# Two sequence mixers in one kernel: x in four loads with the states in time order, part of B turned on TensorE, and a new order of all operations

## The chip, the cores and the metric

The kernel runs on one core of one Trainium2 chip. Its time is the device time of that core in microseconds (us). Of the kernel before, three runs are shown.

## What is computed

Two independent mixers read [1, 2048, 640] inputs in bf16, and their outputs stand side by side in a [1, 2048, 1280] result. Part A is a diagonal complex state-space model (S5): a projection by B, a linear recurrence over the 2048 rows, and a projection by C. Part B is a gated long convolution (H3): a four-tap convolution of k, times v, then a convolution with a filter as long as the sequence, by Fourier transforms, and times q.

```python
# part A
B_bar = ((Lam_bar - 1.0) / Lam)[:, None] * Bmat          # Lam_bar = exp(dt * Lam)
Bu = jnp.einsum("bld,pd->blp", x + 0j, B_bar)
for t in range(L):
    h = Lam_bar[None, :] * h + Bu[:, t, :]
y = 2.0 * jnp.einsum("blp,dp->bld", hseq, Cmat).real + x * Dskip[None, None, :]
# part B
for t in range(ks):                                      # ks = 4
    k_shift = k_shift + k_pad[:, t:t + S, :] * shift_k[:, ks - 1 - t][None, None, :]
kv = k_shift * v
y = irfft(rfft(kv, 2 * S) * rfft(ssm_k, 2 * S), 2 * S)[:, :S] + kv * ssm_D
out = q * y
```

## The kernel before

**Part A.** x comes by eight transposing loads of 256 rows (`load_x`, L525), so that a feature lies on each partition. The rows are taken in residue classes modulo 16, and `base` (L559) multiplies them by B: 400 matmuls of 512 columns, which read x at every second element. The ten state tiles (640 complex states, real and imaginary parts on 128 partitions) stand in `A` as [10 tiles, 16 residues, 130]. The recurrence is done by doubling: `up2`, `up1` and `up0` (with `rmm`, L580) add the state of an earlier residue, times a power of the transition held as a matrix in RR; `coarse` scans the 128 blocks that are left on VectorE (L654 to L665); `down` (L684, its eviction L700 on ScalarE or L702 on VectorE) spreads the result back in four levels. Where ScalarE evicts, an identity matmul (L682) adds the old value. `project` makes 16 output tiles of 128 rows (L719, 20 matmuls of 128x320 each); x times D (L711) is made beforehand from rows that are loaded again (L710), added at the eviction (L721), and stored (L725). B's first 128 rows come plain on ScalarE's DMA queue and are turned by TensorE transposes (L502), the rest in four transposing loads (L493).

**Part B.** k and v come by transposing loads (L774); the convolution is multiplications (L198 on VectorE, L199 on ScalarE), sums (L800) and a product with v (L801), on VectorE or GpSimd. The result goes to a buffer in DRAM (L807) and back in another layout (L817). Two halves of 320 channels follow. A first DFT stage (`s1`, for the filter "h" and the signal "k") is done wide (L836, 16 matmuls) or narrow (L841, 32 matmuls of half the rows and columns), as a flag of the operation says; it is evicted at L846. A second stage (L860, eviction L873) leaves both spectra in SBUF. `product` multiplies them in four blocks of each half: one operation of 128x2560 (L884, on VectorE alone), two in-place products of 128x1280 (L887), a difference (L889) and a sum (L891), these four on VectorE or GpSimd. All blocks share one buffer for the result of L884, so a block's L884 waits for the L889 of the block before. The inverse stages are L905 (eviction L910), which needs all four blocks of its half, and L926 (eviction with times q, L938), then the store.

**Order.** No scheduler runs on the device: each operation is recorded with the engines that could do it, and a table, `ORDER`, lists all operations by number, engine (S for SyncE's DMA queue, A ScalarE, V VectorE, G GpSimd, T TensorE, t for a narrow first stage) and PSUM bank. Each engine does its own in that order, and waits where a footprint in SBUF or a PSUM bank says so. TensorE's results lie in eight banks; an operation takes one or two.

Of the kernel before, what the change touches and what calls it, by code (L numbers as in the profile page):

```python
# [183 lines left out]
for _name, _n in (("A", 10 * 16 * 130), ("BT", 6400), ("RR", 5120), ("W", 4096), ("G", 8192), ("XT", 10240), ("AS", 10240),  # L184
# [153 lines left out]
def params(c):  # L338
# [7 lines left out]
    for k, src in enumerate((lam_re, lam_im, ldt_in)):  # L346
        rows = pr[10 * k:10 * k + 10, :]
        P.add("ld_par", {PSP: .1, PACT: .1}, lambda e, rows=rows, src=src: e.dma_start(
            out=rows.rearrange("p (a b) -> p a b", a=2), in_=bass.AP(src.tensor, 0, [[64, 10], [0, 2], [1, 64]])),
            outs=[tk[:, k:k + 1]], ins=[pr], nbytes=2560)  # L350
# [114 lines left out]
class PartA:  # L465
    def __init__(self, c):
        self.c = c
        v = c.v
        self.A = v("A").rearrange("p (j i s) -> p j i s", j=10, i=16)
        self.BT = []  # L470
        for n, lo in ((2, 0), (4, 1280), (4, 3840)):
# [6 lines left out]
        self.XP = v("XT").rearrange("p (g d s a) -> p d g a s", d=5, g=8, a=2)  # L478
# [3 lines left out]
    def load_B(self, k):  # L482
        c, P = self.c, self.c.P
        n, lo, row = ((2, 0, 0), (4, 1280, 128), (4, 3840, 384))[k]
        raw = c.v("T", 1280, 1280)
        for ri, src in ((0, c.ins["A_B_re"]), (1, c.ins["A_B_im"])):
            if k == 0:
                dst = raw[:, 640 * ri:640 * ri + 640]
                P.add("ld_Braw", {PACT: .1}, lambda e, dst=dst, src=src: e.dma_start(out=dst, in_=src[0:128, :]), outs=[dst], nbytes=128 * 1280)
                continue  # L490
            dst = c.v("BT", lo + 320 * n * ri, 320 * n).rearrange("p (d m) -> p d m", d=5)
            s = src[row:row + 64 * n, :].rearrange("p (d q) -> p d q", q=128)
            P.add(f"ld_B{k}", {PSP: 64 * n * .0055}, lambda e, dst=dst, s=s: e.dma_start_transpose(out=dst, in_=s), outs=[dst],  # L493
                  nbytes=64 * n * 1280)
        if k == 0:
            idn = c.I3[:, 0:128]
            for r in range(2):
                g, out, part = P.group(1), c.v("BT", 640 * r, 640), raw[:, 640 * r:640 * r + 640]

                def mm(e, B, part=part):  # L500
                    for d in range(5):
                        e.transpose(out=B.bitcast(bf16)[:, 128 * d:128 * d + 128], in_=part[:, 128 * d:128 * d + 128], identity=idn)  # L502
                P.add("turn_B", {PPE: .29}, mm, ins=[part, idn], group=g, nmm=5)
                P.add("ev_B", {PDVE: .5, PACT: .7}, lambda e, B, out=out: c.CP[e](out=out, in_=B.bitcast(bf16)[:, 0:640]), outs=[out], group=g)
# [15 lines left out]
    def load_x(self, g):  # L520

        c, P = self.c, self.c.P
        dst = c.v("XT", 1280 * g, 1280).rearrange("p (d t) -> p d t", d=5)
        s = self.x2.rearrange("(s r) (d q) -> r s d q", r=8, q=128)[min(ROW0[2 * g], ROW0[2 * g + 1])]
        P.add(f"ld_x{g}", {PSP: 1.4}, lambda e: e.dma_start_transpose(out=dst, in_=s), outs=[dst], nbytes=256 * 1280)  # L525
# [30 lines left out]
    def base(self, e, o, j, q):  # L556
        for d in range(5):
            for r in range(2):
                e.matmul(o[64 * r:64 * r + 64], lhsT=self.BT[j][:, r, d, :], rhs=self.XP[:, d, 2 * q:2 * q + 2], start=(d == 0),  # L559
                         stop=(d == 4), skip_group_check=True, tile_position=(0, 64 * r))  # L560

    def base_in(self, j, q):
        return [self.BT[j], self.c.v("XT", 2560 * q, 2560)]

    def up2(self, j0, q):
# [4 lines left out]
        def mm(e, B):  # L570
            for a in range(2):
                self.base(e, B[:, 512 * a:512 * a + 512], j0 + a, 2 + q)
        P.add(f"up2{q}_{j0}", {PPE: 10 * .216}, mm, ins=self.base_in(j0, 2 + q) + [self.BT[j0 + 1]], group=g, nmm=20)
        out = self.A[:, j0:j0 + 2, 8 + 4 * q:12 + 4 * q, 0:128]
        P.add(f"ev_up2{q}_{j0}", {PDVE: dve(1024), PACT: act(1024)},
              lambda e, B: c.CP[e](out=out, in_=B.rearrange("p (a i s) -> p a i s", a=2, s=128)), outs=[out], group=g)  # L576

    def rmm(self, e, o, n, j, lo, hi):
# [591 lines left out]
```

## Time and profile before

| | |
|---|---|
| three runs | 198.66, 199.42 and 200.72 us; median 199.42 |
| the profiled execution | span 199.3 us from first to last instruction, 0.1 under the median |
| busy share | TensorE 91%, VectorE 82%, ScalarE 68%, GpSimd 37% |
| mean granted TensorE clock | 0.991 |
| DMA | 30.15 MB, 151 GB/s on average |
| VectorE instructions / GpSimd instructions | 225 / 62 |

In the profile PE is TensorE's matmul stream, PEld its weight loads, DVE VectorE, ACT ScalarE, POOL GpSimd, and SP the queue that issues most DMA. A line such as L887 is a line of the kernel before. A group row gives the line, engine, operation, output and input shape and count, then busy time and the mean of one in ns, then the idle time of the engine just ahead of them with what ended it. A timeline row gives start and duration in us, and in brackets the idle time ahead. Matmuls are pipelined, so that the duration of one is longer than the distance to the next.

### The profile page before, as it was taken

To read this page: it belongs to the slowest core of one execution; us is meant where nothing else is said; L and a number is where in the kernel's file an instruction comes from. 1 tells how busy PE (TensorE), PEld (TensorE's weight loads), DVE (VectorE), ACT (ScalarE), POOL (GpSimd) and SP (SyncE) were. 2 spreads that over 40 slices of the span, in tenths; PEclk is the share of its full clock that TensorE was granted. 3 is DMA by queue.
4 is the path that set the end of the run, shared out by engine and by line. 5 is a ranking of instruction groups with operands and counts; after the bars stand their busy time and mean duration, and the time that the engine had idled before them with its cause. 6 is when DMAs were issued, how large, how long until landed. Compare 5 with 4: busy or idle time off the path is not lost.

```text
span 199.3 us, 7475 instructions
## 1 busy us (share of the span) xinstructions
PE 181.9 (91%) x3324; PEld 123.4 (62%) x3324; DVE 163.0 (82%) x225; ACT 135.8 (68%) x166; POOL 73.1 (37%) x62
## 2 busy tenths in 40 slices
PE   4979999999799999888959988999999999999992
PEld 1545555654468674665738654755767786797771
DVE  4705699599868979999898878989989999997941
ACT  3279988959888689998967889983877290192000
POOL 8399800590060050007270385299250004500050
PEclk9999999999999999999997999999999999999999
DMA  5999999999999999999892799028546732375785
GB/s 107 183 174 134 193 134 163 167 155 178 235 221 288 153 169 157 173 138 116 143 286 55 172 134 138 5 79 125 130 127 140 168 99 72 102 199 135 162 200 139
DMA packets 107738, 30.15 MB, mean 151 GB/s; under 512 B 102586, under 2 KB 107066, under 8 KB 107706
## 3 DMA queue, kind: packets, MB, share of 16 engines
q1 hardware_dynamic: 107418, 29.35, 84.0%
q8 instruction: 26, 0.43, 1.0%
q10 hardware_dynamic: 288, 0.33, 0.6%
q14 instruction: 6, 0.05, 0.1%
HBM read 10.99 MB, written 7.86 MB: 95 GB/s over the span
## 4 chain that ended last, share of the span: by engine, by line
PE 52%; DMA 14%; DVE 11%; ACT 11%; SPq 7%; issue 3%; ACTq 0%; DVEq 0%
PE acc L559 18%; PE acc L719 16%; ACT arena L873 6%; DMA arena<-in_A_x_dram 5%; PE acc L860 4%; PE acc L905 4%; SPq L767 4%; DMA arena<-in_B_k_dram 3%; DMA kv_rows<-arena 2%; ACT arena L846 2%; DMA arena<-in_A_B_re_dram 2%; PE acc L684 2%; PE acc L580 2%; DVE arena L721 2%; PE acc L926 2%
## 5 line engine op out<-in xcount | busy, mean ns | idle before, releaser
L559 PE MATMUL acc<-arena 128*64 128x512 bf16 x400 | 47.3, 389 | 1.5 <-DMA arena<-in_A_B_re_dram 1.1
L719 PE MATMUL acc<-arena 128*128 128x320 bf16 x320 | 45.7, 299 | 0.8 <-ACT arena L846 0.6
L873 ACT CAST arena<-acc 128x960 bf16<-128x960 f32 (+1 forms) x41 | 36.2, 916 | 9.2 <-PE acc L860 7.3
L719 PEld LDWEIGHTS <-arena 128*128 128x128 bf16 x320 | 30.3, 98 | 13.4 <-ACT arena L846 0.8
L559 PEld LDWEIGHTS <-arena 128*64 128x64 bf16 x400 | 24.4, 108 | 21.2 <-issue 2.6
L846 ACT CAST arena<-acc 128x1024 bf16<-128x1024 f32 x29 | 27.7, 1054 | 3.0 <-PE acc L836 2.3
L910 ACT CAST arena<-acc 128x1024 bf16<-128x1024 f32 x17 | 16.2, 1035 | 16.4 <-PE acc L905 16.4
L860 PE MATMUL acc<-arena 128*64 128x160 bf16 x512 | 23.7, 238 | 1.4 <-ACT arena L873 0.8
L887 POOL TENSOR_TENSOR arena<-arena 128x1280 bf16<-128x1280 bf16 x6 | 16.7, 2790 | 20.7 <-DVE arena L884 20.7
L860 PEld LDWEIGHTS <-arena 128*64 128x64 bf16 x512 | 18.3, 111 | 9.2 <-ACT arena L873 3.6
L702 DVE TENSOR_TENSOR arena<-acc,arena 128x1024 bf16<-128x1024 f32 (+1 forms) x15 | 17.2, 1166 | 2.4 <-PE acc L684 2.0
L836 PE MATMUL acc<-arena 128*64 128x128 bf16 x400 | 15.2, 227 | 4.3 <-DVE arena L721 2.1
L721 DVE TENSOR_TENSOR arena<-acc,arena 128x640 bf16<-128x640 f32 x16 | 13.2, 823 | 6.8 <-PE acc L719 5.7
L800 DVE TENSOR_TENSOR arena<-arena 128x2048 bf16<-128x2048 bf16 x14 | 17.1, 1220 | 1.0 <-ACT arena L199 0.8
L836 PEld LDWEIGHTS <-arena 128*64 128x64 bf16 x400 | 12.9, 115 | 6.6 <-DVE arena L721 2.2
L846 DVE CAST arena<-acc 128x1024 bf16<-128x1024 f32 x11 | 13.1, 1219 | 4.5 <-PE acc L836 3.9
L889 POOL TENSOR_TENSOR arena<-arena 128x1280 bf16<-128x1280 bf16 x3 | 7.8, 2609 | 19.6 <-DVE arena L887 19.5
L684 PE MATMUL acc<-arena 128*128 128x512 bf16 (+2 forms) x50 | 12.4, 337 | 0.8 <-ACT arena L873 0.7
L199 ACT ACTIVATE arena<-arena 128x2048 bf16<-128x2048 bf16 (+2 forms) x10 | 11.0, 1110 | 2.7 <-DMA arena<-in_B_k_dram 2.7
L884 DVE TENSOR_TENSOR arena<-arena 128x2560 bf16<-128x2560 bf16 x8 | 11.9, 1489 | 0.5 <-ACT arena L873 0.3
L711 POOL TENSOR_TENSOR arena<-arena 128x640 bf16<-128x640 bf16 x4 | 5.8, 1458 | 17.5 <-DMA arena<-in_A_x_dram 17.5
L576 DVE CAST arena<-acc 128x1024 bf16<-128x1024 f32 x4 | 4.9, 1225 | 8.8 <-PE acc L559 8.8
(143 smaller groups left out, 283.4 us busy)
## 6 DMA issues: line engine op xcount, KB each, us to landing
out_dram<-arena SPq DMA_DIRECT2D x32, 160.0 KB, 2.9
arena<-in_B_ssm_k_dram SPq DMA_DIRECT2D x8, 320.0 KB, 7.1
kv_rows<-arena SPq DMA_DIRECT2D x5, 512.0 KB, 4.0
arena<-kv_rows SPq DMA_DIRECT2D x16, 160.0 KB, 5.0
arena<-in_A_x_dram SPq DMA_DIRECT2D x16, 160.0 KB, 3.5
arena<-in_B_q_dram SPq DMA_DIRECT2D x8, 320.0 KB, 4.6
arena<-in_A_B_im_dram ACTq DMA_DIRECT2D x1, 160.0 KB, 2.5
arena<-in_A_B_re_dram ACTq DMA_DIRECT2D x1, 160.0 KB, 2.7
```

The lines of the kernel that those rows point to most:

```text
L559: e.matmul(o[64 * r:64 * r + 64], lhsT=self.BT[j][:, r, d, :], rhs=self.XP[:, d, 2 * q:2 * q + 2], start=(d == 0), stop=(d == 4), skip_gro ...
L684: e.matmul(B[:, o:o + 128 * k], lhsT=c.RR[:, n, j, :], rhs=A[:, j, q:q + k, 0:128], start=not by_pe, stop=True, skip_group_check=True)
L702: e.tensor_tensor(out=o, in0=b, in1=o, op=ALU.add)
L719: e.matmul(B[:, 512 * b:512 * b + 320], lhsT=lh[j], rhs=self.CT[:, j, 320 * b:320 * b + 320], start=(j == 0), stop=(j == 9))
L721: P.add(f"ev_C{i}", {PDVE: dve(640)}, lambda e, B: e.tensor_tensor(out=ys.rearrange("p (b n) -> p b n", b=2), in0=B.rearrange("p (b n) -> ...
L800: P.add(f"ca{d}_{j}", tt, lambda e: e.tensor_tensor(out=t1, in0=t1, in1=t2, op=ALU.add), outs=[t1], ins=[t1, t2])
L836: e.matmul(B[64 * b:64 * b + 64, 128 * i:128 * i + 128], lhsT=lh[i], rhs=F[:, b, :], start=True, stop=True, tile_position=(0, 64 * b))
L846: P.add(f"e1{what}{hf}_{u}", {PACT: act(1024), PDVE: dve(1024)}, lambda e, B: c.CP[e](out=out, in_=(B.rearrange("p (l n s k) -> p k s l n" ...
L860: e.matmul(B[64 * s:64 * s + 64, 512 * b + 160 * i:512 * b + 160 * i + 160], lhsT=c.W[:, k, 64 * b:64 * b + 64], rhs=self.AS[hf][:, k, 160 ...
L873: c.CP[e](out=out, in_=b.rearrange("p r (k j n) -> p r k j n", k=n, j=4) if nj > 1 else b.rearrange("p r (k x) -> p r k x", k=n))
L887: P.add(f"pq{hf}", n2, lambda e, a=a, b=b: e.tensor_tensor(out=X[:, :, a], in0=X[:, :, a], in1=Yk[:, :, b], op=ALU.mult), outs=[X[:, :, a] ...
L910: P.add(f"er2{hf}_{u}", {PACT: act(1024), PDVE: dve(1024)}, lambda e, B: c.CP[e](out=out, in_=B.rearrange("p (s n b) -> p b s n", s=2, n=4 ...
```

## The change

Five things, of which the last holds the greatest part of the text:

1. x comes in four transposing loads of 512 rows (residue classes modulo 4), and `base` reads each contiguously.
2. The states of a tile stand in `A` as four blocks of 512 in time order (row 4t + r in block r). The first two doubling levels work on contiguous blocks, the third on every second, the fourth on every fourth element; `up0` becomes 8 + 4 + 4 matmuls of 512, 256 and 128 columns, where the latter two write every second and fourth column of a PSUM bank, in place of 8, 12 and 16 of 256, 128 and 128 (beside the 20 of `base`). `coarse` writes its result at every fourth element, and `project` loads its weights at every fourth.
3. B's rows 0 to 255 come plain (four loads on ScalarE's queue) and are turned by 20 TensorE transposes, before 128 rows and 10 transposes; the remaining rows come in two transposing loads in place of four.
4. Three warming matmul groups in place of six.
5. A new `ORDER` throughout: other engines for many operations, 37 of the 40 first DFT stages narrow (before 15), another sequence on every engine. On SyncE's queue the loads of x rows for the first output tiles (L708 now, L710 before) come ahead of the second half's filter loads (L765, before L767), where they stood behind.

Lines move up by one to two: L887, L889 and L891 of before are L885, L887 and L889 now, L884 is L882, L711 is L709, L800 and L801 are L798 and L799, L721 is L719, L938 is L936.

The diff, cut to its core:

```diff
-        self.A = v("A").rearrange("p (j i s) -> p j i s", j=10, i=16)
+        self.A = v("A", 0, 20500).rearrange("p (j x) -> p j x", j=10)
...
-        self.XP = v("XT").rearrange("p (g d s a) -> p d g a s", d=5, g=8, a=2)
+        self.XP = v("XT").rearrange("p (q d t) -> p q d t", q=4, d=5)
...
+        if k == 2:
+            for ri, src in srcs:
...
+                s = src[256:640, :].rearrange("p (d q) -> p d q", q=128)
+                P.add(f"ld_B{k}", {PSP: 1.4}, lambda e, dst=dst, s=s: e.dma_start_transpose(out=dst, in_=s), outs=[dst], nbytes=384 * 1280)
+            return
+        raw, idn = c.v("T", 1280 + 1280 * k, 1280), c.I3[:, 0:128]
...
-        s = self.x2.rearrange("(s r) (d q) -> r s d q", r=8, q=128)[min(ROW0[2 * g], ROW0[2 * g + 1])]
-        P.add(f"ld_x{g}", {PSP: 1.4}, lambda e: e.dma_start_transpose(out=dst, in_=s), outs=[dst], nbytes=256 * 1280)
+        s = self.x2.rearrange("(t r) (d q) -> r t d q", r=4, q=128)[(3, 1, 0, 2)[q]]
+        P.add(f"ld_xp{q}", {PSP: 2.6}, lambda e: e.dma_start_transpose(out=dst, in_=s), outs=[dst], nbytes=512 * 1280)
...
-                e.matmul(o[64 * r:64 * r + 64], lhsT=self.BT[j][:, r, d, :], rhs=self.XP[:, d, 2 * q:2 * q + 2], start=(d == 0),
+                e.matmul(o[64 * r:64 * r + 64], lhsT=self.BT[j][:, r, d, :], rhs=self.XP[:, q, d], start=(d == 0),
...
-        part(f"up0a_{j0}", 256, 256, ((0, 12), (1, 4)), True, A[:, j0:j0 + 2, 2:4, 0:128], None)
-        part(f"up0b_{j0}", 0, 128, ((0, 14), (1, 6), (2, 2)), False, A[:, j0:j0 + 2, 1, 0:128], None)
-        part(f"up0c_{j0}", 128, 128, ((0, 15), (1, 7), (2, 3), (3, 1)), False, self.V[:, j0:j0 + 2, :], None)
+        two = slice(j0, j0 + 2)
+        part(f"up0a_{j0}", slice(0, 512), ((0, slice(1024, 1536)), (1, slice(512, 1024))), True, A[:, two, 1537:2049:2], slice(0, 512, 2))
+        part(f"up0b_{j0}", slice(1, 512, 2), ((2, slice(1537, 2049, 2)),), False, A[:, two, 1538:2047:4], slice(1, 510, 4))
+        part(f"up0c_{j0}", slice(3, 512, 4), ((3, slice(1538, 2047, 4)),), False, self.V[:, two, :], slice(3, 512, 4))
...
-        H = self.A[:, 5 * h:5 * h + 5, 0, 1:129]
+        H = self.A[:, 5 * h:5 * h + 5, 1540:2049:4]
...
-        lh = [A[:, j, i, lo:lo + 128] for j in range(10)]
+        lh = [A[:, j, lo:lo + 509:4] for j in range(10)]
...
-    for k in range(6):
+    for k in range(3):
         a.warm(k)
...
-    "140S0 141G0 147A0 75V0 76S0 77S0 8G0 146A0 7G0 9V0 13G0 59G0 0V0 3T1 5T4 21V0 110V0 14V0 18V0 57V0 4T4 15V0 16V0 100G0 19V0 "
+    "107V0 149A0 72V0 0G0 2T0 95G0 35G0 97G0 3T1 10G0 96G0 131G0 19G0 4G0 56G0 5G0 138G0 12V0 16V0 30V0 47G0 150A0 6V0 73S0 74S0 "
```

What the new table does to GpSimd at the end of its work, where the products are made. Before, from its second L887 to the last L889:

```order
L887 TENSOR_TENSOR arena<-arena 128x8x160
L889 TENSOR_TENSOR arena<-arena 128x8x4x40
L887 TENSOR_TENSOR arena<-arena 128x8x160
L711 TENSOR_TENSOR arena<-arena 128x640
L887 TENSOR_TENSOR arena<-arena 128x8x160
L889 TENSOR_TENSOR arena<-arena 128x8x4x40
L887 TENSOR_TENSOR arena<-arena 128x8x160
L891 TENSOR_TENSOR arena<-arena 128x8x4x40
L887 TENSOR_TENSOR arena<-arena 128x8x160
L889 TENSOR_TENSOR arena<-arena 128x8x4x40
```

Now, the last stretch of the products on GpSimd, eleven rows:

```order
L885 TENSOR_TENSOR arena<-arena 128x8x160
L889 TENSOR_TENSOR arena<-arena 128x8x4x40
L709 TENSOR_TENSOR arena<-arena 128x640
L885 TENSOR_TENSOR arena<-arena 128x8x160
L889 TENSOR_TENSOR arena<-arena 128x8x4x40
L885 TENSOR_TENSOR arena<-arena 128x8x160
L887 TENSOR_TENSOR arena<-arena 128x8x4x40
L885 TENSOR_TENSOR arena<-arena 128x8x160 x2
L889 TENSOR_TENSOR arena<-arena 128x8x4x40 x2
L885 TENSOR_TENSOR arena<-arena 128x8x160
L889 TENSOR_TENSOR arena<-arena 128x8x4x40 x2
```

Over the whole, GpSimd's L887 x6, L889 x3 and L891 x2 of before become L885 x10, L887 x3 and L889 x7, and four L709 stand between them where two L711 did.

VectorE in the same part of the program, the second half's products. Before, from the second block's L884 on:

```order
L884 TENSOR_TENSOR arena<-arena 128x2560
L887 TENSOR_TENSOR arena<-arena 128x8x160 x2
L711 TENSOR_TENSOR arena<-arena 128x640
L721 TENSOR_TENSOR arena<-acc,arena 128x640
L887 TENSOR_TENSOR arena<-arena 128x8x160
L711 TENSOR_TENSOR arena<-arena 128x640
L889 TENSOR_TENSOR arena<-arena 128x8x4x40
L884 TENSOR_TENSOR arena<-arena 128x2560
L721 TENSOR_TENSOR arena<-acc,arena 128x640
L887 TENSOR_TENSOR arena<-arena 128x8x160
L711 TENSOR_TENSOR arena<-arena 128x640
L891 TENSOR_TENSOR arena<-arena 128x8x4x40
```

Now, from the second block's L882 on:

```order
L882 TENSOR_TENSOR arena<-arena 128x2560
L908 CAST arena<-acc 128x256x4
L885 TENSOR_TENSOR arena<-arena 128x8x160
L709 TENSOR_TENSOR arena<-arena 128x640 x2
L719 TENSOR_TENSOR arena<-acc,arena 128x640
L887 TENSOR_TENSOR arena<-arena 128x8x4x40
L882 TENSOR_TENSOR arena<-arena 128x2560
L885 TENSOR_TENSOR arena<-arena 128x8x160
L887 TENSOR_TENSOR arena<-arena 128x8x4x40
L719 TENSOR_TENSOR arena<-acc,arena 128x640
L709 TENSOR_TENSOR arena<-arena 128x640
L936 TENSOR_TENSOR arena<-acc,arena 128x2x8x40
```

Of the products that stood between VectorE's evictions (L721, L938) several have gone to GpSimd; the evictions of the inverse DFT (L908, before L910) stand between the rest.

GpSimd just ahead of the products, in the part of the convolution and the scan (L436, now also L436, spreads the power matrices into RR). Before:

```order
L641 COPY arena<-arena 128x1280
L330 TENSOR_TENSOR arena<-arena 128x1024
L436 TENSOR_TENSOR arena<-arena 128x1280
L800 TENSOR_TENSOR arena<-arena 128x2048
L769 TENSOR_TENSOR arena<-arena 128x80
L887 TENSOR_TENSOR arena<-arena 128x8x160
```

Now:

```order
L330 TENSOR_TENSOR arena<-arena 128x1024
L452 TENSOR_TENSOR arena<-arena 128x1280
L798 TENSOR_TENSOR arena<-arena 128x2048
L436 TENSOR_TENSOR arena<-arena 128x1280 x3
L798 TENSOR_TENSOR arena<-arena 128x2048
L799 TENSOR_TENSOR arena<-arena 128x2048
L709 TENSOR_TENSOR arena<-arena 128x640
L885 TENSOR_TENSOR arena<-arena 128x8x160
```

Two more L436, one more convolution sum (L798) and one product with v (L799) stand ahead of the first L885 there.

128 lines of the change are left out of this document (59 added, 69 removed), and 73 rows, old and new, of the table ORDER.

## The prediction

> **What bounds the kernel now.** I read the head of the page first, then a table of stretches, the chain of waits, and the timelines of VectorE and GpSimd. The page and the table:
>
> ```profile
> span 199.3 us, 7475 instructions
> PE 181.9 (91%) x3324; PEld 123.4 (62%) x3324; DVE 163.0 (82%) x225; ACT 135.8 (68%) x166; POOL 73.1 (37%) x62
> PE 52%; DMA 14%; DVE 11%; ACT 11%; SPq 7%; issue 3%; ACTq 0%; DVEq 0%
> ```
>
> ```profile
> 96.00:173.00 77.00, 71.54 (x1411) 50.66 (x1412) 70.17 (x75) 51.82 (x57) 33.09 (x14) 0.98 0.59 122
> 173.00:199.30 26.30, 22.70 (x564) 17.80 (x564) 17.70 (x21) 6.62 (x7) 2.75 (x2) 1.00 0.67 165
> ```
>
> The busy columns are PE, PEld, DVE, ACT, POOL. TensorE sets the pace with 91%, but in the 77 us in which the frequency products are made VectorE is busy for 70.2 of them too. The span is 199.3 and the median of the shown runs 199.42, so a sum made in the span needs no conversion (0.1).
>
> The timelines show a second limit that no busy column names. VectorE first, then GpSimd:
>
> ```profile
> 42.48 3.24 DVE L801 TENSOR_TENSOR arena<-arena 128x2048 bf16<-128x2048 bf16 x1
> ...
> 97.60 1.49 DVE L884 TENSOR_TENSOR arena<-arena 128x2560 bf16<-128x2560 bf16 x1
> 99.72 2.53 DVE L711 TENSOR_TENSOR arena<-arena 128x640 bf16<-128x640 bf16 x1 [0.63 <-DMA arena<-in_A_x_dram]
> ...
> 129.78 0.82 DVE L887 TENSOR_TENSOR arena<-arena 128x1280 bf16<-128x1280 bf16 x1
> ...
> 136.64 3.48 DVE L702 TENSOR_TENSOR arena<-acc,arena 128x1024 bf16<-128x1024 f32 x3
> ...
> 171.84 0.97 DVE L891 TENSOR_TENSOR arena<-arena 128x1280 bf16<-128x1280 bf16 x1
> 172.73 0.48 DVE L711 TENSOR_TENSOR arena<-arena 128x640 bf16<-128x640 bf16 x1
> ```
>
> ```profile
> 42.31 2.32 POOL L452 TENSOR_TENSOR arena<-arena 128x1280 int32<-128x1280 int32 x1
> ...
> 99.29 2.61 POOL L887 TENSOR_TENSOR arena<-arena 128x1280 bf16<-128x1280 bf16 x1
> ...
> 129.82 3.25 POOL L887 TENSOR_TENSOR arena<-arena 128x1280 bf16<-128x1280 bf16 x1 [4.21 <-DVE arena L884]
> 133.03 2.60 POOL L889 TENSOR_TENSOR arena<-arena 128x1280 bf16<-128x1280 bf16 x1
> 135.60 2.60 POOL L887 TENSOR_TENSOR arena<-arena 128x1280 bf16<-128x1280 bf16 x1
> 138.17 2.61 POOL L891 TENSOR_TENSOR arena<-arena 128x1280 bf16<-128x1280 bf16 x1
> ```
>
> VectorE's scaling of an x tile (L711) takes 0.48 when GpSimd is idle, and 2.53 when it begins 0.43 after a GpSimd product: it ends 0.35 after that product does. L801 at 42.48 needs 3.24, of which 2.15 lie beside a GpSimd instruction. The other way round, GpSimd's product at 129.82 begins beside a VectorE product and takes 3.25 instead of 2.61. But the three L702 at 136.64, which read PSUM, take 3.48 together (1.16 each) beside GpSimd and lose nothing. So an operation of VectorE with SBUF operands alone (I call it a **lock** operation) and any GpSimd operation run one after the other, whole instructions at a time; VectorE's evictions from PSUM run beside GpSimd freely.
>
> **The change, part by part.** Prices by line and shape, GpSimd and then VectorE:
>
> ```profile
> L887 POOL TENSOR_TENSOR arena<-arena 128x1280 bf16<-128x1280 bf16 x6 | 16.7, 2790 | 20.7 <-DVE arena L884 20.7
> L711 POOL TENSOR_TENSOR arena<-arena 128x640 bf16<-128x640 bf16 x4 | 5.8, 1458 | 17.5 <-DMA arena<-in_A_x_dram 17.5
> L800 POOL TENSOR_TENSOR arena<-arena 128x2048 bf16<-128x2048 bf16 x1 | 4.1, 4070 | 17.9 <-DVE arena L198 17.9
> L436 POOL TENSOR_TENSOR arena<-arena 128x1280 bf16<-128x1280 bf16 x1 | 2.5, 2517 | 12.0 <-ACT arena L199 12.0
> ```
>
> ```profile
> L702 DVE TENSOR_TENSOR arena<-acc,arena 128x1024 bf16<-128x1024 f32 x14 | 16.7, 1220 | 2.4 <-PE acc L684 2.0 <-ACT arena L873 0.3
> L800 DVE TENSOR_TENSOR arena<-arena 128x2048 bf16<-128x2048 bf16 x14 | 17.1, 1220 | 1.0 <-ACT arena L199 0.8
> L884 DVE TENSOR_TENSOR arena<-arena 128x2560 bf16<-128x2560 bf16 x8 | 11.9, 1489 | 0.5 <-ACT arena L873 0.3
> L198 DVE TENSOR_SCALAR arena<-arena 128x2048 bf16<-128x2048 bf16 x15 | 11.0, 749 | 0.2
> L887 DVE TENSOR_TENSOR arena<-arena 128x1280 bf16<-128x1280 bf16 x10 | 8.1, 820 | 0.1
> ```
>
> *Products.* Each of the eight blocks needs L884, two L887, L889 and L891; the last three kinds cost 0.82 on VectorE and 2.61 on GpSimd. From the first L884 to the last L891 the old order asks of the lock: GpSimd 11 products x 2.61 + 2 L711 x 1.41 = 31.5; VectorE 8 x 1.49 + 21 x 0.82 + 2 L800/L801 x 1.22 + 8 L711 x 0.48 = 35.4; 67 in all, in the 75.2 us from 97.60 to the last L891, which ends at 171.84 + 0.97 = 172.8. The new order gives GpSimd 20 of the 32 products (10 L887, 3 L889, 7 L891) and 4 L711 in this stretch: 52.2 + 5.6 = 57.8. VectorE keeps 8 x 1.49 + 12 x 0.82 + 4 convolution sums x 1.22 + 2 L198 x 0.75 + 5 L711 x 0.48 = 30.5. Together **88**, less about 3 because neighbours on one engine overlap, by 0.03 on GpSimd (2.60 long, started 2.57 apart) and by 0.09 on VectorE (three L702 of 1.22 in 3.48): 85, so 18 more than before. The bounds: nothing shared costs GpSimd's 57.8 alone; the full exclusion costs 88. I take 85, the lock being what the rows above show each time that the two meet.
>
> *The start of the products.* TensorE's work ahead of them shrinks. The chain of waits gives the projection and the doubling steps, the table by line the first DFT stage:
>
> ```profile
> 7.56 4.82 DMA arena<-in_A_B_re_dram
> ...
> 35.40 0.43 PE acc L580 x4
> 35.83 2.26 PE acc L559 x20
> ...
> 172.96 1.21 PE acc L905 x32
> ```
>
> ```profile
> L836 PE MATMUL acc<-arena 128*64 128x128 bf16 x400 | 15.2, 227 | 4.3 <-DVE arena L721 2.1 <-ACT arena L600 1.2 <-ACT arena L846 0.7
> L841 PE MATMUL acc<-arena 64*64 64x64 bf16 x480 | 6.1, 195 | 0.9 <-ACT arena L846 0.6 <-ACT arena L600 0.2
> ```
>
> L559 reads x at every second element: 2.26 for ten pairs, 0.226 a pair; L580 with contiguous columns takes 0.43 for two, 0.215. Contiguous x saves 0.011 x 200 pairs = 2.2. A wide first-stage operation (16 matmuls) is busy 15.2 / 25 = 0.61, a narrow one (32) 6.1 / 15 = 0.41; 22 more of the 40 become narrow: 22 x 0.20 = 4.4, of which 13 operations, 2.6, lie ahead of the products. The doubling steps and the identity matmuls give some 0.7. The 10 more turnings of B cost up to 1.2, mostly under the 4.82 that TensorE now waits for B by DMA, which is as long for the new queue: I take 0 for the whole start, bounds -1 to +2. So the first product moves from 97.6 to 97.6 - 5.5 = **92**. The lower bound is 88: VectorE also hands over two L436 and two convolution operations, about 4 us of its time. The upper bound is 99.5: these four cost GpSimd 2 x 2.52 + 2 x 4.07 = 13.2 and relieve the lock of 5.8 at most, so up to 7.4 more of it falls into the scan and the convolution ahead of the products.
>
> *Strides.* The Trainium skill, "SBUF — State Buffer", in the box on cachelines under "Door 1", says that bf16 may be read with a stride of up to 8 for free; by it the gain of 2.2 is nothing, where the rows show 0.011 a pair, so they disagree by that much. The same box says that any non-contiguous access of PSUM slows matmuls significantly, which speaks against the doubling steps that now write every second or fourth column of a bank; no run here shows such a write. From the rows: these are 20 matmuls of 256 and 20 of 128 columns, 1.6 us as contiguous ones (0.43 for four of 512 columns, in proportion); at half speed they cost 1.6 more, at full speed 0. C's weights now stand 4 elements apart, 320 loads hidden under matmuls: 0 to 1.5. I take 0 for both.
>
> *From the last product to the end.* The second half's inverse DFT (L905 at 172.96) needs all four blocks of its half. From there to the end it is 26.3 (the second stretch above), five output tiles and the last inverse stage, TensorE at 22.7. The new order has the same ten L905 groups and five tiles behind that point. I keep 26.3.
>
> **The sum.** 92 + 85 + 4 (the lock idle while a product waits for an operand; before it was 75.2 - 67 = 8, and a busier lock idles less) + 26.3 = **207**: slower by 8. TensorE's 7 us of savings turn into waits in front of L905. VectorE is in order, so a lock operation that waits 2.6 holds the evictions behind it, and TensorE, which owns eight banks, stands.
>
> **Rivals.**
>
> *A: GpSimd's share is covered.* If VectorE's evictions fill the time in which GpSimd holds the lock, or the halves leave enough room, TensorE sets the end. For it: TensorE is the 91% engine, VectorE is relieved of nine products, and PSUM evictions do run beside GpSimd. Against: 85 us of lock work must fit between 92 and the last product, which would have to end at 189.9 - 26.3 = 163.6. Another gain goes with it: the loads of x rows for the output tiles now stand ahead of the second half's filter loads on SP, where these rows show TensorE held:
>
> ```profile
> 100.73 0.45 PE L841 MATMUL acc<-arena 64*64 64x64 bf16 x32
> 103.24 0.70 PE L836 MATMUL acc<-arena 128*64 128x128 bf16 x16 [2.06 <-DVE arena L721]
> ```
>
> The time: 199.3 - 2.2 - 4.4 - 0.7 - 2.1 = 189.9. It holds in full if the stretch from first to last product takes no more than 72 us, and some of it is left up to 81.
>
> *B: both cancel.* The first product at 88 and no idle lock: 88 + 85 + 26.3 = 199.3. For it: the old order did with 8 us of idle lock what a tighter one may do with none. Against: in-order queues of both engines would have to mesh all the way.
>
> *C: the lock bites earlier too.* The convolution's GpSimd operations of 4.07 hold VectorE in the scan, TensorE waits for the scan, and the first product comes at 99.5: 99.5 + 85 + 4 + 26.3 = 214.8; with the strides' 1.6 it is 216.4. For it: L801 at 42.48 lost 2 us in that way. Against: GpSimd's rows there end ahead of the products if their operands come as early as VectorE's did.
>
> *D: the new order is only a re-arrangement* with the same lock demand. The order's rows exclude that: 20 products for 11.
>
> **How the numbers follow.** Forecast 0.57, A 0.23, B 0.10, C 0.10. The forecast's own range is 201 to 213 (first product 90 to 95, idle lock 0 to 7). The range for 8 in 10 reaches up into C and down into the space between A and B: 192 to 215. About 1% is what a measurement of this kernel can tell from no change (the three runs span 198.66 to 200.72). Faster by over 1%: A and a part of B, 0.25. Within 1%: the rest of B and the forecast's edge, 0.09. Slower: 0.66.
>
> **What would show it.** In the changed profile GpSimd should be busy for some 110 us; its L885, L887 and L889 should stand back to back with a mean near 2.6 to 2.9; VectorE's L882, L885 and L709 should show durations of 2 to 4 us where they wait; the first L882 should begin at 88 to 97 and the second half's inverse DFT near 181, with TensorE's idle time ahead of the inverse DFT grown and released by GpSimd. L559's pair should cost 0.215, and narrow operations replace the wide. I am wrong if VectorE's and GpSimd's SBUF operations overlap at their normal durations, or if GpSimd's products end ahead of 165: then A holds.

## The result, and the profile after

The changed kernel takes 245.13 us (median of 4 runs, 244.57 to 246.36), the kernel before 199.53 in the same comparison; the ratio is 1.242, with a 95% interval of 1.230 to 1.254. It was forecast slower, at 207; it is slower by 46 and not by 8. The ratios here compare undisturbed executions alone, while the medians are over all of them, which matters for the kernel before, whose runs lie between 195.6 and 201.0 us. The page of the changed kernel:

```profile
span 243.3 us, 7977 instructions
PE 187.1 (77%) x3566; PEld 127.5 (52%) x3566; DVE 213.2 (88%) x231; ACT 129.9 (53%) x149; POOL 118.6 (49%) x75
PE 19%; DVE 15%; issue 3%; ACT 2%; POOL 2%; DMA 1%; DVEq 0%
```

VectorE has become the busiest engine: 213.2 us in 231 instructions, where 225 took 163.0 before. TensorE's share fell from 91% to 77%. Cut at the first L882 and at the end of the last L889, 209.3 (VectorE's last L887 ends 0.7 later; columns as in the prediction's table: stretch, length, PE, PEld, DVE, ACT, POOL, granted clock, DMA share, GB/s):

```profile
0.00:117.90 117.90, 91.61 (x1450) 53.18 (x1451) 105.28 (x141) 72.71 (x89) 51.99 (x49) 0.90 0.85 142
117.90:209.30 91.40, 70.53 (x1519) 53.24 (x1518) 89.05 (x70) 49.31 (x53) 63.80 (x24) 0.93 0.48 97
209.30:243.30 34.00, 24.96 (x600) 21.10 (x598) 18.87 (x23) 7.89 (x8) 2.80 (x2) 0.90 0.54 133
```

| stretch | before | forecast | after | after less before |
|---|---|---|---|---|
| to the first product | 97.6 | 92 | 117.9 | +20.3 |
| products | 75.2 | 85 + 4 | 91.4 | +16.2 |
| behind the last product | 26.5 | 26.3 | 34.0 | +7.5 |
| span | 199.3 | 207 | 243.3 | +44.0 |

The products came out 2 us above the forecast. The stretch ahead of them is 26 us off, the one behind 8.

What happened ahead of them is plainest between 17 and 37 us. VectorE's timeline of the changed kernel:

```profile
17.66 3.07 DVE L436 TENSOR_TENSOR arena<-arena 128x1280 bf16<-128x1280 bf16 x1
20.66 1.86 DVE L269 TENSOR_SCALAR arena<-arena 128x32 int32<-128x32 int32 x1
22.55 1.83 DVE L272 TENSOR_SCALAR arena<-arena 128x64 int32<-128x64 int32 x1
24.30 1.21 DVE L578 CAST arena<-acc 128x1024 bf16<-128x1024 f32 x1
...
27.91 1.86 DVE L413 TENSOR_TENSOR arena<-arena 128x20 f32<-128x20 f32 x1
29.75 0.07 DVE L647 MEMSET arena<- 128x10 bf16 x1
29.81 1.82 DVE L415 TENSOR_TENSOR arena<-arena 128x20 f32<-128x20 f32 x1
31.66 2.24 DVE L417 TENSOR_TENSOR arena<-arena 128x20 f32<-128x20 f32 x1
...
35.71 1.22 DVE L578 CAST arena<-acc 128x1024 bf16<-128x1024 f32 x1
```

GpSimd beside it:

```profile
17.49 1.89 POOL L330 TENSOR_TENSOR arena<-arena 128x1024 int32<-128x1024 int32 x1
19.35 3.14 POOL L291 TENSOR_TENSOR arena<-arena 128x1024 int32<-128x1024 int32 x1
22.45 1.89 POOL L330 TENSOR_TENSOR arena<-arena 128x1024 int32<-128x1024 int32 x1
...
27.85 1.89 POOL L291 TENSOR_TENSOR arena<-arena 128x1024 int32<-128x1024 int32 x1
29.70 1.89 POOL L330 TENSOR_TENSOR arena<-arena 128x1024 int32<-128x1024 int32 x1
31.55 2.31 POOL L452 TENSOR_TENSOR arena<-arena 128x1280 int32<-128x1280 int32 x1
```

And TensorE:

```profile
9.28 8.82 PE L558 MATMUL acc<-arena 128*64 128x512 bf16 x80 [1.33 <-DVE arena L256]
25.57 8.09 PE L558 MATMUL acc<-arena 128*64 128x512 bf16 x60 [7.46 <-DVE arena L578]
36.98 2.35 PE L558 MATMUL acc<-arena 128*64 128x512 bf16 x20 [3.32 <-DVE arena L578]
```

L413, L415 and L417 work on 20 elements a partition; each takes about 2 us, and L413 and L417 end 0.03 to 0.04 after the GpSimd instruction ahead of it (27.91 + 1.86 = 29.77 against 27.85 + 1.89 = 29.74). Two of L578's evictions stand behind such instructions in VectorE's queue, the PSUM banks stay full, and TensorE stands for 7.5 and 3.3 us. The first of these stands is paid twice, as the granted clock (the column behind the five busy ones) shows:

```profile
16.00:18.00 2.00, 2.00 (x20) 1.10 (x16) 1.90 (x2) 1.85 (x4) 2.00 (x2) 1.00 0.98 71
26.00:28.00 2.00, 2.00 (x12) 0.92 (x10) 1.97 (x3) 0.00 (x0) 2.00 (x3) 0.50 1.63 124
96.00:98.00 2.00, 1.82 (x40) 1.06 (x38) 1.97 (x3) 1.15 (x2) 1.80 (x1) 0.50 0.95 161
```

In the 2 us from 16 TensorE runs 20 matmuls of 512 columns at full clock, behind the stall only 12 at 0.50. The clock is back at 1.00 from 28.5 us on; behind the 3.3 us stand (37 to 39 us) it stays at 1.00.

The third of these rows belongs to a second meeting, in the scan right ahead of the products:

```profile
88.11 4.06 POOL L798 TENSOR_TENSOR arena<-arena 128x2048 bf16<-128x2048 bf16 x1 [31.50 <-DVE arena L198]
96.19 4.05 POOL L799 TENSOR_TENSOR arena<-arena 128x2048 bf16<-128x2048 bf16 x1 [4.03 <-DMA arena<-in_B_v_dram]
```

```profile
89.35 4.26 DVE L667 TENSOR_TENSOR arena<-arena 128x640 bf16<-128x640 bf16 x1
...
96.83 3.77 DVE L660 TENSOR_TENSOR arena<-arena 128x640 bf16<-128x640 bf16 x1
```

```profile
93.76 0.74 PE L686 MATMUL acc<-arena 128*128 128x128 bf16 x5 [3.54 <-DVE arena L667]
...
101.88 1.07 PE L839 MATMUL acc<-arena 64*64 64x64 bf16 x64 [2.20 <-DVE arena L700]
```

Without GpSimd beside it L667 takes 1.60 (at 106.01) and L660 0.49 (at 80.92). The evictions behind them wait, TensorE stands for 3.5 and 2.2 us, and its clock is 0.50 from 93.3 to 107.0.

### The profile page after: what moved, and what is told of

It reads as the page before. It is cut to its first block, busy times and chain, and to the rows that moved or that the text cites. A ratio compares the mean times of both kernels' runs of the same rounds, so it can differ in the third digit from the quotient of the medians.

```text
span 243.3 us, 7977 instructions
## 1 busy us (share of the span) xinstructions
PE 187.1 (77%) x3566; PEld 127.5 (52%) x3566; DVE 213.2 (88%) x231; ACT 129.9 (53%) x149; POOL 118.6 (49%) x75
## 5 line engine op out<-in xcount | busy, mean ns | idle before, releaser
L558 PE MATMUL acc<-arena 128*64 128x512 bf16 x400 | 47.1, 389 | 13.7 <-DVE arena L578 12.2
L885 POOL TENSOR_TENSOR arena<-arena 128x1280 bf16<-128x1280 bf16 x10 | 29.1, 2910 | 34.8 <-ACT arena L552 17.6
L844 ACT CAST arena<-acc 128x1024 bf16<-128x1024 f32 x37 | 35.6, 1025 | 19.2 <-PE acc L839 14.6
L558 PEld LDWEIGHTS <-arena 128*64 128x64 bf16 x400 | 24.1, 113 | 33.8 <-DVE arena L578 14.2
L798 POOL TENSOR_TENSOR arena<-arena 128x2048 bf16<-128x2048 bf16 x2 | 8.1, 4070 | 42.3 <-DVE arena L198 31.5
L908 ACT CAST arena<-acc 128x1024 bf16<-128x1024 f32 x16 | 15.7, 1020 | 23.8 <-PE acc L903 23.8
L700 DVE TENSOR_TENSOR arena<-acc,arena 128x1024 bf16<-128x1024 f32 (+2 forms) x18 | 21.9, 1227 | 3.3 <-PE acc L686 3.2
L889 POOL TENSOR_TENSOR arena<-arena 128x1280 bf16<-128x1280 bf16 x7 | 20.3, 2894 | 8.7 <-DVE arena L885 8.4
L858 PEld LDWEIGHTS <-arena 128*64 128x64 bf16 x512 | 19.7, 115 | 8.7 <-DVE arena L719 1.9
L709 POOL TENSOR_TENSOR arena<-arena 128x640 bf16<-128x640 bf16 x7 | 10.5, 1500 | 20.5 <-DMA arena<-in_A_x_dram 20.5
L839 PEld LDWEIGHTS <-arena 64*64 64x64 bf16 x1184 | 13.4, 119 | 13.3 <-DVE arena L767 4.4
L839 PE MATMUL acc<-arena 64*64 64x64 bf16 x1184 | 15.6, 206 | 6.0 <-DVE arena L767 3.6
L719 DVE TENSOR_TENSOR arena<-acc,arena 128x640 bf16<-128x640 f32 x16 | 13.2, 829 | 7.7 <-PE acc L717 7.3
L903 PE MATMUL acc<-arena 64*128 64x128 bf16 x320 | 13.0, 241 | 8.1 <-DVE arena L719 5.8
L798 DVE TENSOR_TENSOR arena<-arena 128x2048 bf16<-128x2048 bf16 x13 | 18.3, 1405 | 0.4
L903 PEld LDWEIGHTS <-arena 64*128 64x128 bf16 x320 | 11.8, 148 | 9.3 <-DVE arena L719 6.1
L198 DVE TENSOR_SCALAR arena<-arena 128x2048 bf16<-128x2048 bf16 (+2 forms) x22 | 15.5, 716 | 0.3
```

The costliest lines, as they stand in the source:

```text
L700: e.tensor_tensor(out=x, in0=b, in1=x, op=ALU.add)
L709: P.add(f"xd{i}", {PDVE: dve(640, .52), PPOOL: 1.5}, lambda e: e.tensor_tensor(out=ys, in0=ys, in1=c.DR, op=ALU.mult), outs=[ys], ins=[ys, ...
L798: P.add(f"ca{d}_{j}", tt, lambda e: e.tensor_tensor(out=t1, in0=t1, in1=t2, op=ALU.add), outs=[t1], ins=[t1, t2])
L839: e.matmul(B[64 * b:64 * b + 64, 512 * l + 64 * i:512 * l + 64 * i + 64], lhsT=lh[i][ps], rhs=F[ps, b, 64 * l:64 * l + 64], start=True, st ...
L844: P.add(f"e1{what}{hf}_{u}", {PACT: act(1024), PDVE: dve(1024)}, lambda e, B: c.CP[e](out=out, in_=(B.rearrange("p (l n s k) -> p k s l n" ...
L858: e.matmul(B[64 * s:64 * s + 64, 512 * b + 160 * i:512 * b + 160 * i + 160], lhsT=c.W[:, k, 64 * b:64 * b + 64], rhs=self.AS[hf][:, k, 160 ...
```

## The experiments

Two theories went into them. LOCK: an operation of VectorE with SBUF operands alone and a GpSimd operation run one after the other, VectorE's queue is in order, so evictions behind such an operation keep TensorE waiting, and the new order makes them meet far more. LAYOUT, a rival: the new arrangement of x and of the states costs the time itself. ORDER and others stand in the expectations. To separate code and order, a table was written for the changed code with the old sequence, engines and banks; the loads and turnings that have no counterpart stand where their relatives stood.

### The old order on the changed code, and two halves

`old_order`, first line of the table:

```diff
-    "107V0 149A0 72V0 0G0 2T0 95G0 35G0 97G0 3T1 10G0 96G0 131G0 19G0
+    "137S0 138G0 144A0 150A0 72V0 73S0 74S0 5G0 143A0 149A0 4G0 6V0 10G0
```

> The changed code (four x loads, states in time order, 256 rows of B turned) with the old order, operation by operation; x loads, B loads and turnings stand where their counterparts stood. Theory LOCK (an operation of VectorE with SBUF operands and any GpSimd operation run one after the other, and the new order makes them meet far more): all of the loss is the order's, so 195 to 199 us, the projection 0.01 a pair cheaper. Rival LAYOUT (strided weights, strided PSUM writes, longer x loads cost the time): 215 us or more.

Measured: 208.83 (four runs, 203.18 to 210.88), neither. Most of the loss is the order's, but even the lowest run lies 4 to 5 us above the kernel before. The profiled run is one of the long ones (210.57): TensorE stands for 4.3 us up to 45.96 behind an eviction (L844) in VectorE's queue, the first product comes at 109.7, and the products take 70.8.

`old_head` (the old order up to the first product, then what is left of the new):

```diff
     ... 479T6 445A4 439V0 468T2 469A2
-    [rest of the old order]
+    480A6 328T4 329V4 691G0 455T4 332T0 456A4 333V0 450V0 330T0 ...
```

> The changed code, the old order up to the first frequency product, the new order for all that is left. LOCK: first product at 96 to 99, products for about 91 us, 34 us behind them: 221 to 226 us. LAYOUT: as the changed kernel, 240 to 247. If only the head of the new order is bad: 196 to 200.

Measured: 234.13; first product at 108.4, products 89.3, behind them 33.8.

`new_head` (the complement):

```diff
     ... 260A0 252A2 262A4 436A0 268V6
-    [rest of the new order]
+    17V0 435V0 437G0 459T4 460A4 477T2 478V2 700S0 421G0 434S0 ...
```

> The complement: the new order up to the first frequency product, the old order for the rest. LOCK: first product at 116 to 120, products for 75 to 78 us, 26 us behind: 217 to 224 us. If only the products of the new order are bad: 196 to 202.

Measured: 229.11; first product at 127.0, products 72.7, behind them 27.8. The two later stretches follow their order, whichever head is in front: 89 to 91 and 34 with the new, 71 to 73 and 28 with the old. The heads came out 9 and 7 us behind the late end of what was expected: with the old head, as in `old_order`, by something that the changed code brings.

`old_setup` (the old order only up to the first L582):

```diff
     ... 193T4 194A4 195T6 196A6 127V0
-    [rest of the old order]
+    206A0 68G0 61G0 116V0 118V0 117V0 119V0 120V0 125V0 122V0 ...
```

> The changed code, the old order only to the end of the first doubling level's matmuls (tables, parameters, loads, first projection), the new order for the rest. LOCK, in the form that small setup operations of VectorE wait behind table operations of GpSimd and hold the evictions: TensorE's 12 us of waits for the L578 evictions go to under 4, first product at 100 to 108, 225 to 235 us. Rival: the loss ahead of the products is the scan's and the convolution's (three GpSimd operations of 4 us): first product stays at 114 to 120, 240 to 247 us.

Measured: 240.14, first product at 112.1: between the two. TensorE's waits for the L578 evictions were 6.2 us in place of 12.2, now for ScalarE's and not under 4 (all waits ahead of L558: 10.4 in place of 13.7). The seam moved a part of the wait to another engine; it doesn't tell the theories apart.

### The table products, and evictions on ScalarE

`no_tables` cuts eight GpSimd products of the Fourier tables to 8 columns; the other columns are left out.

```diff
-  e.tensor_tensor(out=qc, in0=qc, in1=bc(f41s, [128, 1024]), op=ALU.mult)
+  e.tensor_tensor(out=qc[:, 0:8], in0=qc[:, 0:8], in1=bc(f41s, [128, 8]), op=ALU.mult)
...
-  out=qc.rearrange("p (k b c) -> p k b c", k=8, b=2),
+  out=qc[:, 0:8].rearrange("p (b c) -> p b c", b=2),
```

> The changed kernel with eight GpSimd table products (L291, L330) cut from 1024 columns to 8; the tables of the Fourier stages are wrong thereby, all other work is done. LOCK: VectorE's small setup operations no longer wait 1.6 us each, TensorE's 12 us of waits for the L578 evictions fall to under 4, first product at 103 to 110, 229 to 237 us. Rival ORDER (TensorE's sequence and its banks alone make the stalls): 242 to 247 us, the waits as before.

Measured: 233.65 (ratio 1.187, 1.177 to 1.197); first product at 105.9, 12.0 earlier, and all of it stays to the end (span 230.8, 12.5 less). The same VectorE instructions (lines two higher), which there ran from L306 at 26.93 to L754's end at 34.28, now run from 20.33 to 21.49:

```profile
20.33 0.26 DVE L308 TENSOR_SCALAR arena<-arena 128x192 int32<-128x192 int32 x1
20.50 0.17 DVE L415 TENSOR_TENSOR arena<-arena 128x20 f32<-128x20 f32 x1
...
20.71 0.18 DVE L417 TENSOR_TENSOR arena<-arena 128x20 f32<-128x20 f32 x1
...
22.92 1.22 DVE L580 CAST arena<-acc 128x1024 bf16<-128x1024 f32 x1
```

L413 of the changed kernel is L415 here: 1.86 against 0.17. TensorE's waits for that eviction (PE rows) are 0.6 us in place of 12.2. LOCK is confirmed for this stretch, with its size.

`ev_act` gives ScalarE the nine evictions that VectorE had:

```diff
-  198V0 206V4 204V6 188V4 192V2 232V6 190V2 240V6 208V2
+  198A0 206A4 204A6 188A4 192A2 232A6 190A2 240A6 208A2
```

> The changed kernel with the nine evictions of the first two doubling levels that VectorE had given to ScalarE, nothing else. LOCK: the evictions no longer queue behind locked VectorE operations, TensorE's early waits fall by 8 us or more: 233 to 239 us. ORDER: banks are freed no earlier, 242 to 247 us.

Measured: 247.48. LOCK's number was wrong, and ORDER's 242 to 247 nearly came out. L558 now waits 7.5 us for ScalarE's L578 and 5.5 for its L844. In the first of these waits (4.4 us, up to 26.89) ScalarE's queue itself stands behind a table function that waits 3.7 us for VectorE's small operations (L307 for L306), so that moving the eviction doesn't go around the lock there. Ahead of the 5.5 us ScalarE is busy with four other table functions (L296, L334, 49.7 to 53.7); as far as the rows show, that part is not the lock's.

### The products

`prod_dve` puts all 20 GpSimd products on VectorE, in the same places:

```diff
-  452G0 453G0 451G0 463G0 464G0 462G0 465G0 473G0 476G0 484G0 487G0 610G0 611G0 609G0 620G0 623G0 612G0 631G0 634G0 645G0
+  452V0 453V0 451V0 463V0 464V0 462V0 465V0 473V0 476V0 484V0 487V0 610V0 611V0 609V0 620V0 623V0 612V0 631V0 634V0 645V0
```

> The changed kernel with all 20 GpSimd products on VectorE, in the same places of the order. LOCK: each costs the shared path 0.8 in place of 2.6; the stretch of the products falls from 91 to 78 to 82 us (VectorE's own work), 231 to 236 us. Without a lock VectorE, 213 us busy already, gets 16 us more work: 253 to 262 us.

Measured: 239.27 (ratio 1.216, 1.209 to 1.223), 3 us above LOCK's numbers and 14 below the others: 5.9 faster than the changed kernel, where a VectorE without a lock would have lost 8 or more. The stretch of its products:

```profile
116.30:205.80 89.50, 67.74 (x1512) 54.04 (x1519) 85.70 (x95) 49.71 (x53) 4.37 (x3) 0.93 0.50 99
```

Here 95 VectorE instructions take 85.7 us, with next to no GpSimd beside them; in the changed kernel 70 take 89.05. So GpSimd relieved VectorE of 20 products, 16.4 us of work, and all of it came back as waits. But the stretch hardly shrank, 89.5 for 91.4: without any lock VectorE's own work in this order fills it. The group rows of the changed kernel show the waits:

```profile
L885 POOL TENSOR_TENSOR arena<-arena 128x1280 bf16<-128x1280 bf16 x10 | 29.1, 2910 | 34.8 <-ACT arena L552 17.6 <-DVE arena L882 14.7 <-PE acc L858 2.4
L889 POOL TENSOR_TENSOR arena<-arena 128x1280 bf16<-128x1280 bf16 x7 | 20.3, 2894 | 8.7 <-DVE arena L885 8.4
...
L709 DVE TENSOR_TENSOR arena<-arena 128x640 bf16<-128x640 bf16 x9 | 11.3, 1263 | 0.0
L887 DVE TENSOR_TENSOR arena<-arena 128x1280 bf16<-128x1280 bf16 x5 | 11.3, 2250 | 0.0
```

VectorE's L887 takes 2.25 on average for 0.82 of work, L709 1.26 for 0.48, GpSimd's products 2.9 for 2.6: both sides wait.

`old_pool20` puts the 20 products on GpSimd in the old order:

```diff
-  453V0 451V0 474G0 462V0 486G0 465V0 ... 454G0 611V0 609V0 620V0 623V0 631V0 612V0 644G0 645V0
+  453G0 451G0 474V0 462G0 486V0 465G0 ... 454V0 611G0 609G0 620G0 623G0 631G0 612G0 644V0 645G0
```

> The changed code in the old order, but with the 20 products on GpSimd that the new order has there (11 in the old). LOCK: the stretch from first to last product goes from 75 to 88 to 93 us, 209 to 216 us. Without a lock: GpSimd takes nine products off a VectorE that is 90% busy there, 190 to 198 us.

Measured: 218.48 (ratio 1.110, 1.098 to 1.123); the stretch from first to last product is 84.5 us in place of `old_order`'s 70.8 (`old_order_no_tables`, below, gives 70.8 too). Nine products moved, 13.7 us lost; the prediction's arithmetic gives 9 x (2.61 - 0.82) = 16.1. That GpSimd takes work off a busy VectorE is excluded for this stretch.

### The operations just ahead of the products

`conv_dve` puts three L436, an L798 and the L799 of GpSimd on VectorE:

```diff
-  128G0 130G0 157G0 430G0 431G0
+  128V0 130V0 157V0 430V0 431V0
```

> The changed kernel with five GpSimd operations that stand ahead of the products (three L436, one L798, one L799) on VectorE, in the same places. LOCK: VectorE gets 6.9 us of work of its own and loses some 10 us of waits behind them, the scan no longer stands for 4.3 + 3.8 us, and TensorE's clock stays up: first product at 108 to 114, 233 to 240 us. If VectorE's own load decides there: no gain or a loss, 243 to 250 us.

Measured: 242.21; first product at 115.2. TensorE's two waits for L667 fall from 4.4 to 2.2 us in all, but the gain is 3, short of LOCK's 233 to 240 and just below the other's 243 to 250.

`no_tables_conv` has this edit and that of `no_tables` together:

> Both edits: the eight table products cut to 8 columns (wrong tables) and the five operations on VectorE. LOCK: the two collisions lie in different stretches and add up: first product at 94 to 101, 220 to 228 us. If something else holds the start (loads, TensorE's sequence): first product stays at 104 to 107 as with the tables alone, 229 to 235 us.

Measured: 232.02; first product at 105.2, as with the tables alone. The two do not add up: with the tables gone VectorE is still busy for 88.6 us ahead of that product, 11.9 more than ahead of it in the kernel before (76.7): among them nine of the first 15 evictions, where it had four. Its own load may be the limit then; but the old order on the same code, with the same cut, reaches that product no earlier than 104.4 (`old_order_no_tables`, below), so that the new order has about 1 us left to explain.

### The layout

`old_order_no_tables` has the old order and the cut tables, `before_no_tables` is the kernel before with the same cut (in both the other columns are left out):

> The changed code in the old order, with the eight GpSimd table products cut to 8 columns (wrong tables). LOCK: the 4.3 us stall at 42 us and the half-speed spell behind it came from table products that met VectorE's convolution; they go, 193 to 198 us and level with before_no_tables. LAYOUT: the stall was only a part, it stays 4 us or more above before_no_tables.

> The kernel before with the same cut (wrong tables): the control. It met the lock only at 42.5 us among these (2.0 us, then a wait of 1.2): 1 to 3 us faster than before.

Measured: 205.36 (204.66 to 207.93) and 199.09 (196.17 to 200.64); against the kernel before 1.043 (1.035 to 1.051) and 1.001 (0.995 to 1.007). So LAYOUT holds too: the changed code costs some 8 us in the old order (3.5 to 5.1%), without a stall of note (clock 0.996), and the first product comes 7.0 later (104.4 against 97.4). The control, which was to gain 1 to 3, gained nothing: its single collision was not worth its size. Rows of TensorE, and one of VectorE, `old_order_no_tables` first:

```profile
L584 PE MATMUL acc<-arena 128*64 128x256 bf16 x20 | 3.0, 403 | 0.2 <-ACT arena L628 0.2
L688 PE MATMUL acc<-arena 128*128 128x128 bf16 x10 | 2.5, 296 | 0.0
L584 PE MATMUL acc<-arena 128*64 128x128 bf16 x20 | 2.1, 302 | 0.3 <-ACT arena L628 0.2
L688 PE MATMUL acc<-arena 128*128 128x256 bf16 x10 | 2.0, 276 | 0.0
L669 DVE TENSOR_TENSOR arena<-arena 128x640 bf16<-128x640 bf16 x2 | 3.2, 1608 | 0.0
```

```profile
L582 PE MATMUL acc<-arena 128*64 128x128 bf16 x140 | 5.2, 220 | 0.0
L582 PE MATMUL acc<-arena 128*64 128x256 bf16 x40 | 3.0, 272 | 0.0
L686 PE MATMUL acc<-arena 128*128 128x256 bf16 x10 | 2.1, 273 | 0.1
L686 PE MATMUL acc<-arena 128*128 128x128 bf16 x10 | 1.3, 219 | 0.0
L667 DVE TENSOR_TENSOR arena<-arena 128x640 bf16<-128x640 bf16 x2 | 1.0, 494 | 0.0
```

The doubling matmuls that write every second PSUM column take 403 ns in place of 272, those that write every fourth 302 in place of 220; the first spreading level, which reads every fourth element of SBUF, 296 in place of 219, while reading every second costs next to nothing (276 for 273). With 60 of 512 columns the doubling steps are busy for 8.2 + 3.0 + 2.1 = 13.3 us against 3.0 + 3.0 + 5.2 = 11.2. With that level's identity matmuls (2.4 for 1.4) the three add 4.3 us of busy time to TensorE. VectorE's last step of the scan, which now writes every fourth element (item 2 of the change; L669, before L667), takes 1.61 us in place of 0.49, twice, and TensorE stands 0.34 us for the first of them and 0.93 for an eviction behind the second. How the rest of the 7 comes about was not tried, nor were the three warming groups fewer (item 4): the first 20 matmuls of L560 take 4.5 us here, their counterparts in `before_no_tables` 2.5.

### Single edits of the kernel before

`before_narrow` sets the flag of 22 more first stages:

```diff
-  184T2 172T0 178T0 188T4 174T2 176T4 186T2 402T4 ... 597T0 601T2 595T2
+  184t2 172t0 178t0 188t4 174t2 176t4 186t2 402t4 ... 597t0 601t2 595t2
```

> The kernel before, with the first DFT stage narrow where the changed kernel has it so (37 of 40 in place of 15), nothing else. If the 22 x 0.20 us of TensorE time are on the path: 4 us faster than before. If TensorE waits for VectorE and ScalarE anyway: within 1%.

Measured: 198.97, ratio 1.012 (1.003 to 1.020): not a gain. TensorE's busy time in L836 and L841 falls as forecast, from 21.3 to 16.4 us, but L841 alone now waits 7.1 us where the two waited 5.2; 4.2 of them are put down to issue (nothing that the profile shows held the engine) where it was 0.

`before_narrow_ldr` also moves one load (693) ahead of the filter loads:

```diff
-  ... 315V0 316V0 422S0 420S0 421S0 ... 414T0 415A0 693S0 408T4
+  ... 315V0 316V0 693S0 422S0 420S0 421S0 ... 414T0 415A0 408T4
```

> As before_narrow, and the load of the first output tile's x rows goes ahead of the second half's four filter loads on SyncE's queue. If TensorE's wait of 2.1 us behind the first output tile's eviction was that load: 2 to 3 us faster than before_narrow, its half-speed spell after the wait gone too. If not: the same.

Measured: 199.60, ratio 1.020 (1.015 to 1.025). `before_ldr` is this move alone:

> The kernel before, only the load of the first output tile's x rows ahead of the second half's filter loads. LOCK: VectorE's L711 then comes ahead of GpSimd's first product and no longer waits 2.1 us behind it with L721 in its queue, and TensorE's 2.1 us wait and the half-speed spell go: 1 to 3 us faster than before. Rival: the time is given back before the second half's products end: within 1%.

Measured: 196.64 (12 runs, 195.06 to 197.98), where the kernel before gave 199.09 (29 runs, 195.86 to 201.03); ratio 0.997 (0.992 to 1.001). TensorE's 2.1 us wait is gone, but the ratio does not tell a gain from none, and LOCK's 1 to 3 us are not shown. `before_fix2` swaps two VectorE operations besides:

```diff
-  234T2 371S0 368V0 178T0 179V0 372V0
+  234T2 371S0 178T0 179V0 368V0 372V0
```

> As before_ldr, and on VectorE the product with v that stood 2.0 us behind a GpSimd table operation (L801 at 42.48) goes behind the next eviction. LOCK: the eviction comes 1.6 us earlier, TensorE's 1.2 us wait shrinks: 0 to 1.5 us faster than before_ldr.

Measured: 196.40 (195.16 to 197.60); ratio 0.996 (0.992 to 1.001), no different from `before_ldr`. No version tried beats the kernel before by more than is told from nothing.

## Why the prediction was wrong

**The direction and the lock: right.** VectorE and GpSimd excluded each other in every stretch looked at, and the products took 91.4 us for a forecast of 89. The reason was only half of it: `prod_dve` shows that VectorE's own work in the new order would fill 89.5 of them without GpSimd. The sum of 85 counted VectorE's SBUF operations alone (30.5) and left out its evictions, so that the nearness of the two numbers is in part luck. The lock's part is that GpSimd's help was worth nothing.

**The step that failed: "I take 0 for the whole start, bounds -1 to +2", and with it "the first product moves to 92", upper bound 99.5.** It came at 117.9. I had priced the GpSimd operations that changed engine (13.2 us, "up to 7.4 more") and not the table products that stayed on GpSimd and were now met by other VectorE operations. A small operation waits there as long as a large one: 0.17 us of work cost 1.9, several times in a row. `no_tables` puts this at 12 us. The order alone shows which operations stand between the evictions on VectorE and which stand on GpSimd in the same stretch; I compared only the products so. Rival C named the mechanism, for the convolution and the scan, and stopped at 214.8; that meeting is there too (L667 and L660 above), but `conv_dve` makes it worth 3 us.

**The strides: "I take 0 for both"; gains of 2.2 in the projection and "some 0.7" in the doubling steps.** In the old order the changed code costs some 8 us. The first gain did come (ten pairs in 2.16 us, before 2.26). The second came out the other way: the doubling steps and the identity matmuls take 3.1 us more, the spreading level 1.2. VectorE's strided write (2.2 us) was in no term. The Trainium skill's sentence on PSUM ("SBUF — State Buffer", the box on cachelines) was the better guide: 403 for 272 ns and 302 for 220 are its slowing. Its stride of up to 8 bf16 for free does not hold at 4 elements here (296 for 219), and nearly holds at 2 (276 for 273) in these rows.

**The clock: left out.** The mean granted clock fell from 0.99 to 0.91. The prediction had a row with its trace (the 2.06 us wait at 103) and no price for the half-speed spell behind it; the 7.5 us of waiting that ended at 25.6 were followed by 2.9 us at 0.50, and the waits in the scan lie beside 13.7 us of it. Ahead of the first product TensorE is busy at 0.50 for 2.9 + 10.5 + 3.4 = 16.8 us (the last from 110.4 to 113.8), so that by an estimate up to half of that, 8 us, went there; no run separates it.

**Behind the last product: 26.3 forecast, 34.0 measured.** Ten L905 groups and five tiles did stand there, as counted. The stores were not counted. SyncE's last issues:

```profile
228.09 7.17 SPq L948 DMA_DIRECT2D out_dram<-arena  x9
235.35 0.96 SPq L723 DMA_DIRECT2D out_dram<-arena  x1
...
238.79 1.12 SPq L723 DMA_DIRECT2D out_dram<-arena  x2
```

Nine stores of part B stand ahead of the last output tiles'. The last eviction ends at 237.0, the span at 243.3: 6.3 us, before 2.7 (196.65 to 199.3). Another 1.9 pass between the last L889 and the first L903 (211.18), and from there to the last matmul it is 25.0 against 22.8, part of it at half clock. `old_head` keeps this stretch at 33.8, `new_head` gives 27.8: it belongs to the new order's end.

**Rival A's savings** were not there either: narrow stages gain nothing (`before_narrow`), so the 4.4 in its time, 2.6 of which the forecast took too, was no path time. Busy time per operation is no saving where an eviction sets the pace.

What stays open: by the profiles the 20.3 us ahead of the products split into 7.0 from the code (97.4 to 104.4, old order, tables cut), 1.4 from the new order with the tables cut (to 105.9) and 12.0 from the table products in the new order (to 117.9); these are single profiles. The old order with its tables comes to 104.2 in `old_pool20`, 108.4 in `old_head` and 109.7 in `old_order`, whose heads are the same, so that what the tables cost there changes from run to run. Of the code's 7.0 only a part is traced.

## What to carry to other kernels

Before a share of VectorE's work goes to GpSimd, add up both engines' SBUF work in the stretch as if one engine did it: that sum, with the waits of small operations as long as GpSimd's instructions, bounds the stretch, as does the whole work of VectorE, its evictions included, and evictions from PSUM must not queue behind it. Check it for set-up code too, where instructions of 0.2 us meet instructions of 2 us. When a table of orders is replaced, each stretch has to be priced for what meets there, not only for what changed engine, down to the last stores on the queue.

## What the runs showed of the hardware

- A VectorE instruction of 128x20 f32 took 1.86 us beside GpSimd's 1.89 us integer products and 0.17 without them. Single-source operations wait likewise (L269, 128x32 int32: 1.86 where it took 0.24 in the kernel before). Not every operation with SBUF operands alone does: a memset of 128x10 (L647) took 0.07 us beside the product at 29.70, an operation of one element a partition (L249 at 143.21) 0.14 beside GpSimd's L709.
- TensorE's half clock comes in spells, in the changed kernel of 3.4, 6.8 and 13.7 us, each beside a stand; the length of the stand alone doesn't tell. The stand of 7.5 us up to 25.6 had one from 21.7 to 28.5, the 3.3 us up to 37.0 had none, and behind 1.1 us up to 110.2 the clock was 0.50 from 110.4 to 113.8. In 2 us TensorE ran 20 matmuls of 512 columns at 1.00 and 12 at 0.50.
- A matmul that writes every second column of a PSUM bank took 403 ns for 256 columns (272 contiguous); one that reads every fourth bf16 of SBUF 296 ns for 128 columns (219), every second 276 for 256 (273). VectorE's 128x640 sum that writes every fourth element took 1.61 us (0.49 contiguous). Weight loads of every fourth element took 115 ns in place of 98 and stayed hidden: the matmuls over them took 300 and 299.
